# A second attention group moved back by one dense block, key scaling ahead of a weight conversion, and two steps' expert splits at fixed places

## The chip, the core and the metric

The kernel runs on one core of a Trainium2 chip. The metric is the device time of one execution in microseconds, here the median of three timed runs. A further execution was profiled; the rows below come from it.

## What is computed

A gated linear attention over 4 x 8 heads, 768 positions and 48 dimensions, then a dense layer with squared ReLU over 3072 tokens of 384 values (inner size 2048), then a routed layer in which each token goes to one of 8 experts (inner size 1024). All is in float32; the dense weights arrive as 64-bit numbers.

```
state = f[t] * state + k[t] v[t]^T;  y[t] = q[t] state      # per head
x   = relu(x @ w_in) ** 2 @ w_out                           # 3072 x 384, inner 2048
e   = argmax(x @ w_gate);  p = softmax(x @ w_gate)[e]
out = p * (relu(x @ w1[e]) @ w2[e])                         # 8 experts, inner 1024
```

## The kernel before

**Attention and dense layer.** The sequence is cut into 24 chunks of 128 tokens; three chunks make a dense group `g` of 384 tokens, 0 to 7. Each group goes through 16 blocks `i` of 128 inner columns: `moe_h` (PE, L394 in group 0 and L404 later, tile `ph`), `moe_act` (ScalarE L410 and L411 make `gg`, L415 its rounded part `gh`, VectorE L417 the rest `gl`) and, two blocks later, `moe_out` (PE, L434, three tiles `po`). The attention of group g + 1 is woven into the blocks of group g by `attention_group`, a generator that is resumed after each `moe_h` (`late` 0) and after each `moe_out` (`late` 1). For its m-th chunk it issues the scores (`pk` L256, `pa` L263) and the masked product `at` (L270) at block 5m, the decays of the next chunk (scans L215 and L224) one block later, the outputs (L299, L309, L319) two, and the scaling of the next chunk's queries and keys (`scale_qk`, VectorE L234 to L236) three blocks later. The scaled keys are the input of `pk`. At the head of the program the scaling of chunk 3 is issued by itself, behind `convert_job(2)`.

**Conversion of the weights.** In group 0 the dense weights are narrowed from 64-bit numbers by VectorE, in 16 jobs of three operations each (L166, L169, L172), two blocks' worth of `w_in` (even jobs) or `w_out` (odd jobs) at a time. Job n frees one of three staging buffers, into which SP then loads job n + 3 (L184). h(2j) and h(2j + 1) of group 0 read the tile of job 2j. When the last job is issued the staging pool is closed and a table `wgb` is loaded (L784) into its place; SP's queue has the next chunks' loads and the transposed group (`xT`, L335) behind it. From group 1 on, each weight is used as a rounded high part `w_hi` and a rest `w_lo`, and each product takes three matmuls.

**Expert steps.** The routed layer runs as 16 fixed steps on gathered tokens, of two kinds, "D" with 256 tokens and "S" with 128. A step has 8 blocks: hidden matmuls (L981, or L969 in an S step's first half), `hh` (ScalarE L985), `hl` (VectorE L986) and output matmuls two blocks later (L1001, `qo` in a D step, `qs` in an S step). The weights of a step are 8 raw tiles (`load_w`, SP, L634, `raw<-w_e`); `split_part` makes the high part on ScalarE (L612) and the rest (L613) on VectorE or, in the steps, on either VectorE or GpSimd. A split of raw tile j frees it, and `load_w` for the next step follows. Steps write their split weights alternately into two sets, `wst_[0]` (which was the dense `w_in`) and `wst_[1]` (dense `w_out`). The splits of step 0 and some of step 1 are made while the last blocks of group 7 still run. Where the splits of later steps go is planned by `split_plan`, which steps through the blocks with assumed durations; a tile is `ready` 4.0 after its release, and for step `NEARLY` (2) not before a given block of step 1, since its expert number comes from the tables that `final_tables` builds in steps 0 and 1 (`sel` L668, `pi` L672). The last group's routing (`route(7)`, L546 to L554) runs there too.

**Order.** Through the dense groups PE, ScalarE, VectorE and GpSimd run in the order of the program text (`by_hand`); SP's order, and the order of engines that are not named in a later `manual_schedule`, is the scheduler's. In steps 0 and 1 only PE was in program order.

Of the kernel before, what the change touches and what calls it, by code (L numbers as in the profile page):

```python
# [41 lines left out]
NEARLY = 2  # L42
# [14 lines left out]
def gla_moe_moe_kernel(ctx: ExitStack, tc: tile.TileContext, qk, ft, vt, w_in, w_out, w_gate, w_gateT, w_e, q, k, v, f_logit, out, dbg=None):  # L57
# [106 lines left out]
    def narrow(dst, w):  # L164
        low, high = w[..., 0], w[..., 1]
        nc.vector.tensor_scalar(  # L166
            out=dst, in0=high, scalar1=3, scalar2=0x3FFFFFFF, op0=ALU.logical_shift_left, op1=ALU.bitwise_and
        )
        nc.vector.scalar_tensor_tensor(  # L169
            out=dst, in0=high, scalar=0xC0000000, in1=dst, op0=ALU.bitwise_and, op1=ALU.bitwise_or  # L170
        )
        nc.vector.scalar_tensor_tensor(  # L172
            out=dst, in0=low, scalar=29, in1=dst, op0=ALU.logical_shift_right, op1=ALU.bitwise_or
        )
# [4 lines left out]
    def stage_job(n):  # L179
        if n < len(jobs):  # L180
            which, j = jobs[n]
            src = w_out[:, 2 * j : 2 * j + 2, :] if which else w_in[:, :, j * 256 : (j + 1) * 256]
            t = stg.tile([128, WP], I64, tag="stg", name="stg")
            nc.sync.dma_start(out=t.rearrange("p (a b) -> p a b", a=src.shape[1]), in_=src)  # L184
            staged[n] = t

    def convert_job(n):
        if n < len(jobs):
            w_raw[jobs[n]] = t = wlp.tile([128, WP], F32, tag="w", name="w_raw")
            narrow(t.bitcast(U32), staged.pop(n).bitcast(U32).rearrange("p (b two) -> p b two", two=2))  # L190
            stage_job(n + 3)
# [37 lines left out]
    def scale_qk(c):  # L229
        t, pr, _ = ld_t[c]  # L230
        tl, _ = prep_t[c]
        pairs = lambda a: a.rearrange("p (a b) -> p a b", a=4)
        qd, kd = t[:, 0], t[:, 1]
        nc.vector.tensor_tensor(out=kd, in0=kd, in1=pairs(tl[:, 1:FL])[:, :, 1:], op=ALU.mult)  # L234
        nc.vector.tensor_tensor(out=qd, in0=qd, in1=pairs(pr[:, 0 : FL - 1])[:, :, 1:], op=ALU.mult)
        nc.vector.tensor_tensor(out=pmin[0:PR], in0=pmin[0:PR], in1=tl[:, 1:FL:SEG], op=ALU.min)  # L236

    def x_tiles(g):
        xT = (
            xhp.tile([128, 3, G], F32, tag="xl", name="xT0")  # L240
            if g == 0
            else xp.tile([128, 3, G], F32, tag="xT", name="xT")
        )
        x_t[g] = xT, xp.tile([128, G], F32, tag="xT3", name="xT3")
# [93 lines left out]
    def state(c, pu):  # L338
        if pu is None:
            return  # L340
        wn = wst[(c + 1) % 2][:, :, 0:D]
        emb = prep_t[c + 1][1][:, :, None].to_broadcast([PR, 4, D])
        if c % CPB == 0:
            nc.vector.tensor_tensor(out=wn, in0=pu[0:PR], in1=emb, op=ALU.mult)
        else:
            nc.vector.tensor_tensor(out=wn, in0=pu[0:PR], in1=wst[c % 2][:, :, 0:D], op=ALU.add)
            nc.vector.tensor_tensor(out=wn, in0=wn, in1=emb, op=ALU.mult)
# [12 lines left out]
    def attention_group(g):  # L360
        for m in range(GC):
            c = g * GC + m
            b = 5 * m
            while not (yield) == (b, 1):
                pass
            if m == 0:
                x_tiles(g)
            if 4 < c + 2 < NCH:
                load_chunk(c + 2)
            scores(c)  # L370
            masked(c)
            sigmoid(c + 1)
            while not (yield) == (b + 1, 0):
                pass
            if c + 1 < NCH:
                decays(c + 1)
            while not (yield) == (b + 2, 1):
                pass
            state(c, outputs(c))
            while not (yield) == (b + 3, 0):  # L380
                pass
            if c + 1 < NCH:
                scale_qk(c + 1)
        while not (yield) == (14, 0):
            pass
        split_x(g)
        yield
# [210 lines left out]
    convert_job(1)  # L598
    decays(3)
    state(2, pu)  # L600
    convert_job(2)
    scale_qk(3)
    job = 3

    ph2 = ExitStack()
    early = {}
    rawt, xg = [], []
    wst_ = []
    ids_t, esi_t, reg_t, x_s, out_t = {}, {}, {}, {}, {}

    def split_part(hi, lo, src, eng=nc.vector):
        nc.scalar.activation(out=hi, in_=src, func=AF.Copy)  # L612
        eng.tensor_tensor(out=lo, in0=src, in1=hi.bitcast(F32), op=ALU.subtract)  # L613
# [15 lines left out]
    def load_w(s, j):  # L629
        if s >= NALWAYS:  # L630
            return
        if s not in reg_t:
            reg_t[s] = nc.sync.value_load(esi_t[s], min_val=0, max_val=NE - 1)
        nc.sync.dma_start(out=rawt[j], in_=w_e[bass.ds(reg_t[s] * 128, 128), j * WP : (j + 1) * WP])  # L634
# [66 lines left out]
    def open_right():  # L701
# [42 lines left out]
        load_x(0)  # L744
        load_x(1)

    pend = []
    rt_gen = None

# [15 lines left out]

    for g in range(NG):
        att = Piece(attention_group(g + 1)) if g + 1 < NG else None
        if g == NG - 1:
            right = open_right()
        for i in range(NF):  # L770
            ph = moe_h(g, i)
            if att:
                att.at(i, 0)
            if rt_gen and 2 <= i <= 10 and g < NG - 1:
                next(rt_gen, None)
            if g == 0 and job < len(jobs):
                convert_job(job)
                job += 1
                if job == len(jobs):
                    phs.close()  # L780
                    wgp = pha.enter_context(tc.tile_pool(name="wgp", bufs=1, side="right", reuse_waits="tile"))
                    wgb = [wgp.tile([128, NE, DM], F32, name="wgb")]
                    early["ab"] = [wgp.tile([128, NBLK + SB], F32R, name=f"ab{m}") for m in range(GC)]
                    nc.sync.dma_start(out=wgb[0], in_=w_gateT[None, :, :].to_broadcast([128, NE, DM]))  # L784
            pend.append((g, i, *moe_act(g, ph)))
            n = g * NF + i - 8
            split_job(n)
            if n == len(jobs) - 1:
                wst_.extend([[w_hi[w][:, j], w_lo[w, j]] for j in range(NP)] for w in range(2))
            if len(pend) > 2:  # L790
                done = flush_one()
                if done is not None:
                    rt_gen = route(done)
                    next(rt_gen)
            if att:
                att.at(i, 1)
            if g == NG - 1:
                if i < 2:
                    next(right, None)

                for j in {5: [0], 7: [1], 9: [2], 10: [3], 11: [4], 13: [5], 15: [6, 7]}.get(i, ()):
                    split_part(*wst_[0][j], rawt[j])
                    load_w(1, j)
                if i == 13:
                    prep_step(0, *early["x0"])
            if rt_gen and i >= 2 and (i > 10 or g == NG - 1):
                next(rt_gen, None)
        if rt_gen:
            for _ in rt_gen:
                pass  # L810
            rt_gen = None
# [130 lines left out]
        nc.vector.tensor_tensor(out=need, in0=need, in1=over[:, 1:2], op=ALU.add)  # L942
        nc.vector.scalar_tensor_tensor(out=tot, in0=need, scalar=0.0, in1=bad, op0=ALU.max, op1=ALU.add)

    early["split"], early["ready"] = [], False
    SPLITS = split_plan()


# [123 lines left out]
        if s < NEARLY:  # L1072
            next(fin, None)

    with tc.manual_schedule(engines={mybir.EngineType.PE}):
        left = run_steps(0, NEARLY, hook, flush=False)
    with tc.manual_schedule(engines={mybir.EngineType.PE, mybir.EngineType.Activation}):
        run_steps(NEARLY, NALWAYS, pend=left)
# [11 lines left out]
def split_plan():  # L1090
    slots, clock = [], 0.0
    for s, kind in enumerate(KINDS[:NALWAYS]):
        for i in range(8):
            slots.append((clock, s, i))
            clock += 2.0 if kind == "D" else 1.2
    begin = {(s, i): t for t, s, i in slots}
    ready, plan = {(1, j): 0.0 for j in range(8)}, {}

    def release(s, j, t):
        if s < NALWAYS:  # L1100
            ready[s, j] = max(t + 4.0, begin[1, 2] if s == NEARLY else 0.0)

    for t, s, i in slots:
        if KINDS[s] == "S" and i % 2:
            release(s + 1, i // 2, t)
        due = []
        for (u, j), r in ready.items():
            if (KINDS[u] == "S" and j < 4) or r > t or begin[u - 1, 2 if j == 7 else 0] > t:
                continue
            due.append((begin[u, 2 * j if j < 4 else min(2 * j - 6, 7)], u, j))  # L1110
        due.sort()
        for n, (end, u, j) in enumerate(due[:2]):
            if n and end > t + 6.0:
                break
            del ready[u, j]
            plan.setdefault((s, i), []).append((u, j))
            release(u + 1, j, t)
    return plan
# [252 lines left out]
```

## Time and profile before

| | us |
|---|---|
| median of 3 timed runs | 824.01 |
| lowest and highest | 823.91, 825.7 |
| the profiled execution | 823.52 |
| its span | 821.7 |
| PE busy | 785.1 (96% of the span) |
| VectorE, ScalarE, GpSimd busy | 548.8, 414.2, 159.9 |

Span is the time from the first to the last instruction of the profiled execution. PE is TensorE's matmul queue; a matmul counts as busy on a lower clock too, so a slow stretch doesn't show in this share.

### The profile page before, as it was taken

Reading aid. Unit: us, or ns where it says so; the run is one execution under the profiler, and the core shown is the slowest. Engines: PE = TensorE matmul, PEld = TensorE weight load, DVE = VectorE, ACT = ScalarE, POOL = GpSimd, SP = SyncE. Lnnn points to the kernel's source line nnn. Section 1 sums busy time; section 2 is a strip of 40 time slices with the busy share of each in tenths; the row PEclk is TensorE's granted clock in tenths of the full one; section 3 lists DMA queues with packets and bytes.
Section 4 is the critical chain, followed back from the end, with each engine's and each line's share of the span. In section 5 each row is a group of like instructions: output and inputs, shape, how many; then the busy total and the mean of one; then the engine's idle time right before and its main releaser. Section 6 shows DMA issues by size and latency. Waiting matters only on the chain.

```text
span 821.7 us, 15286 instructions
## 1 busy us (share of the span) xinstructions
PE 785.1 (96%) x5681; PEld 729.6 (89%) x5681; DVE 548.8 (67%) x1266; ACT 414.2 (50%) x830; POOL 159.9 (19%) x158
## 2 busy tenths in 40 slices
PE   5799999999999999999999999989999999999995
PEld 4566679999999999999999999989999899898995
DVE  7979779768768767767767654568566545656641
ACT  2233466455455454454455454753465465555651
POOL 2000000000000000000000011212656466555551
PEclk9899999999999999999999999999999999999998
DMA  9886321112131121130120015314666766758640
GB/s 266 238 266 179 126 47 52 45 53 56 43 88 38 49 63 45 46 98 25 45 69 1 2 43 205 107 59 168 238 210 223 255 218 206 268 177 277 203 143 29
DMA packets 40563, 102.09 MB, mean 124 GB/s; under 512 B 5630, under 2 KB 9442, under 8 KB 40352
## 3 DMA queue, kind: packets, MB, share of 16 engines
q1 hardware_dynamic: 36896, 91.57, 36.3%
q0 software_dynamic: 3584, 9.46, 3.1%
q8 instruction: 47, 0.77, 0.4%
q14 instruction: 36, 0.29, 0.1%
HBM read 91.31 MB, written 10.24 MB: 124 GB/s over the span
## 4 chain that ended last, share of the span: by engine, by line
PE 76%; DVE 8%; issue 6%; DMA 5%; ACT 4%; POOL 1%; SPq 0%; POOLq 0%; DVEq 0%; ACTq 0%
PE po L434 22%; PE ph L404 20%; PE qo L1001 8%; PE ph L981 8%; DVE w_lo L613 4%; PE ph L394 4%; DMA raw<-w_e 3%; PE pa L263 3%; PE py L319 3%; ACT w_hi L612 2%; PE ph L969 1%; PE py L299 1%; PE pu L309 1%; PE qs L1001 1%; DMA xT<-xT 1%
## 5 line engine op out<-in xcount | busy, mean ns | idle before, releaser
L410 ACT ACTIVATE gg<-ph 128x384 f32<-128x384 f32 x128 | 62.7, 490 | 180.8 <-PE ph L404 128.3
L417 DVE TENSOR_TENSOR gl<-gg,gh 128x384 fp32r<-128x384 f32 x112 | 63.4, 566 | 84.4 <-ACT gh L415 83.2
L404 PE MATMUL ph<-xh,w_lo 128*128 128x384 f32 x336 | 118.7, 353 | 0.9 <-ACT gg L410 0.9
L434 PE MATMUL po<-w_hi,gl 128*128 128x384 f32 x336 | 113.8, 339 | 2.2 <-DVE gl L417 2.2
L404 PE MATMUL ph<-xl,w_hi 128*128 128x384 f32 x336 | 114.4, 340 | 0.6 <-DVE xl L162 0.6
L404 PE MATMUL ph<-xh,w_hi 128*128 128x384 f32 x336 | 113.9, 339 | 0.0
L434 PE MATMUL po<-w_hi,gh 128*128 128x384 f32 x336 | 113.7, 338 | 0.0
L434 PE MATMUL po<-w_lo,gh 128*128 128x384 f32 x336 | 113.2, 337 | 0.0
L613 DVE TENSOR_TENSOR w_lo<-raw,w_hi 128x768 fp32r<-128x768 f32 x63 | 94.4, 1500 | 24.0 <-ACT w_hi L612 18.2
L613 POOL TENSOR_TENSOR w_lo<-raw,w_hi 128x768 fp32r<-128x768 f32 x49 | 91.1, 1875 | 82.8 <-ACT w_hi L612 80.4
L612 ACT ACTIVATE w_hi<-raw 128x768 fp32r<-128x768 f32 x112 | 93.8, 839 | 19.8 <-DMA raw<-w_e 19.6
L986 DVE SCALAR_TENSOR_TENSOR hl<-ph,hh 128x256 fp32r<-128x256 f32 (+1 forms) x128 | 48.8, 387 | 78.8 <-ACT hh L985 76.3
L985 ACT ACTIVATE hh<-ph 128x256 fp32r<-128x256 f32 (+1 forms) x128 | 45.2, 356 | 97.5 <-PE ph L981 72.4
L708 POOL MEMSET xg<- 128x385 f32 x4 | 1.5, 422 | 466.9 <-DVE gl L417 466.9
L981 PE MATMUL ph<-xh,w_lo 128*128 128x256 f32 x288 | 82.8, 288 | 5.9 <-DVE w_lo L613 5.9
L458 DVE SCALAR_TENSOR_TENSOR junk<-rows,wgb 128x384 f32<-128x384 f32 x144 | 80.0, 555 | 3.3
L981 PE MATMUL ph<-xl,w_hi 128*128 128x256 f32 x288 | 81.4, 283 | 0.0
L981 PE MATMUL ph<-xh,w_hi 128*128 128x256 f32 x288 | 81.1, 282 | 0.0
L411 ACT ACTIVATE gg<-gg 128x384 f32<-128x384 f32 x128 | 67.2, 525 | 4.0
L404 PEld LDWEIGHTS ph<-xh,w_lo 128*128 128x128 f32 x336 | 63.0, 187 | 6.9 <-issue 3.1
L1001 PE MATMUL qo<-w_hi,hl 128*128 128x384 f32 x192 | 66.4, 346 | 1.7 <-DVE hl L986 1.3
L434 PEld LDWEIGHTS po<-w_hi,gl 128*128 128x128 f32 x336 | 63.3, 189 | 2.8 <-DVE gl L417 2.5
(236 smaller groups left out, 1653.9 us busy)
## 6 DMA issues: line engine op xcount, KB each, us to landing
raw<-w_e SPq DMA_DIRECT2D x128, 384.0 KB
qk<-qk SPq DMA_DIRECT2D x46, 192.0 KB
v<-vt SPq DMA_DIRECT2D x24, 256.0 KB
stg<-w_in SPq DMA_DIRECT2D x8, 768.0 KB
stg<-w_out SPq DMA_DIRECT2D x8, 768.0 KB
f<-ft SPq DMA_DIRECT2D x24, 226.2 KB
xs<-rows SPq DMA_DIRECT2D x8, 577.5 KB
wgb<-w_gateT SPq DMA_DIRECT2D x1, 1536.0 KB
```

Source lines behind the costliest of these rows:

```text
L404: nc.tensor.matmul(ph, lhsT=w[:, sl], rhs=x[:, k, :], start=(n == 0), stop=(n == 8))
L410: nc.scalar.activation(out=gg, in_=ph, func=AF.Relu)
L411: nc.scalar.activation(out=gg, in_=gg, func=AF.Square)
L417: nc.vector.tensor_tensor(out=gl, in0=gg, in1=gh.bitcast(F32), op=ALU.subtract)
L434: nc.tensor.matmul(po[m], lhsT=a[:, sl], rhs=w[:, ws], start=(i == 0 and n == 0), stop=(i == NF - 1 and n == len(terms) - 1),)
L458: nc.vector.scalar_tensor_tensor(out=junk, in0=rows[:, m, 0:DM], scalar=1.0, in1=wgb[0][:, e, :], op0=ALU.mult, op1=ALU.mult, accum_out=lg ...
L612: nc.scalar.activation(out=hi, in_=src, func=AF.Copy)
L613: eng.tensor_tensor(out=lo, in0=src, in1=hi.bitcast(F32), op=ALU.subtract)
L981: nc.tensor.matmul(ph, lhsT=wslice(s, w, (i * 3 + k) * 128, 128), rhs=x[:, k, :], start=(n == 0), stop=(n == 8))
L985: nc.scalar.activation(out=hh, in_=ph, func=AF.Relu)
L986: nc.vector.scalar_tensor_tensor(out=hl, in0=ph, scalar=0.0, in1=hh.bitcast(F32), op0=ALU.max, op1=ALU.subtract)
L1001: nc.tensor.matmul(out_t[s][m], lhsT=x[:, sl], rhs=wslice(s, w, 3 * F2 + i * DM, DM), start=(i == 0 and n == 0), stop=(i == 7 and n == 2),)
```

## The change

Three edits. The attention of group 1 (in group 0's blocks) has its chunks at blocks 1, 6 and 10, not 0, 5 and 10. `scale_qk(3)` is issued ahead of `convert_job(2)`. The splits of steps 0 and 1 that fall into group 7 are listed by a table `AHEAD` (block: step and tile): all eight of step 0 and six of step 1, all on VectorE; the planner starts with what is left, step 2's tiles are ready at block 4 of step 1, and ScalarE too keeps the program order in steps 0 and 1.

```
     def attention_group(g):
         for m in range(GC):
             c = g * GC + m
-            b = 5 * m
+            b = (1, 6, 10)[m] if g == 1 else 5 * m
...
     state(2, pu)
+    scale_qk(3)
     convert_job(2)
-    scale_qk(3)
...
+    AHEAD = {4: [(0, 0)], 5: [(0, 1)], 6: [(0, 2)], 7: [(1, 0)], 8: [(0, 3), (1, 1)], 9: [(1, 2)], 10: [(0, 4)]}
+    AHEAD |= {11: [(1, 3)], 12: [(0, 5)], 13: [(1, 4)], 14: [(0, 6)], 15: [(0, 7), (1, 5)]}
...
-                for j in {5: [0], 7: [1], 9: [2], 10: [3], 11: [4], 13: [5], 15: [6, 7]}.get(i, ()):
-                    split_part(*wst_[0][j], rawt[j])
-                    load_w(1, j)
+                for t, j in AHEAD.get(i, ()):
+                    split_part(*wst_[t][j], rawt[j])
+                    if t == 0:
+                        load_w(1, j)
...
-    early["split"], early["ready"] = [], False
+    early["split"], early["ready"] = [j for js in AHEAD.values() for t, j in js if t == 1], False
...
-    with tc.manual_schedule(engines={mybir.EngineType.PE}):
+    with tc.manual_schedule(engines={mybir.EngineType.PE, mybir.EngineType.Activation}):
         left = run_steps(0, NEARLY, hook, flush=False)
...
-    ready, plan = {(1, j): 0.0 for j in range(8)}, {}
+    ready, plan = {(1, j): 0.0 for j in (6, 7)}, {}
...
-            ready[s, j] = max(t + 4.0, begin[1, 2] if s == NEARLY else 0.0)
-
+            ready[s, j] = max(t + 4.0, begin[1, 4] if s == NEARLY else 0.0)
+
+    for j in range(6):
+        release(NEARLY, j, 0.0)
```

Between chunk 2's state and chunk 3's `at`, VectorE had this order (`wst` is the attention's state, `stg` a staged weight, `qk` the chunk's queries and keys):

```order
L346 TENSOR_TENSOR wst_106<-pu,wst_105 112x4x48
L347 TENSOR_TENSOR wst_106<-wst_106,em 112x4x48
L166 TENSOR_SCALAR w_raw<-stg 128x768
L169 SCALAR_TENSOR_TENSOR w_raw<-stg,w_raw 128x768
L172 SCALAR_TENSOR_TENSOR w_raw<-stg,w_raw 128x768
L234 TENSOR_TENSOR qk_148<-qk_148,tl 112x512
L235 TENSOR_TENSOR qk_148<-qk_148,f 112x512
L236 TENSOR_TENSOR pmin<-pmin,tl 112x4
```

and now has this, with two more conversions (the same three rows) in front of `at`:

```order
L347 TENSOR_TENSOR wst_106<-wst_106,em 112x4x48
L234 TENSOR_TENSOR qk_148<-qk_148,tl 112x512
L235 TENSOR_TENSOR qk_148<-qk_148,f 112x512
L236 TENSOR_TENSOR pmin<-pmin,tl 112x4
L166 TENSOR_SCALAR w_raw<-stg 128x768
L169 SCALAR_TENSOR_TENSOR w_raw<-stg,w_raw 128x768
L172 SCALAR_TENSOR_TENSOR w_raw<-stg,w_raw 128x768
```

The three rows of the scaling went ahead of the three of conversion 2. In the same stretch PE's first dense blocks and chunk 3's scores were in this order:

```order
L394 MATMUL ph<-xT_186,w_raw 128x384 x3
L256 MATMUL pk<-ident,qk_148 128x112 x4
L263 MATMUL pa<-qk_148 128x128 x8
L394 MATMUL ph<-xT_186,w_raw 128x384 x6
L434 MATMUL po_489<-w_raw,gg 128x384
```

and are in this one now:

```order
L394 MATMUL ph<-xT_186,w_raw 128x384 x6
L256 MATMUL pk<-ident,qk_148 128x112 x4
L263 MATMUL pa<-qk_148 128x128 x8
L394 MATMUL ph<-xT_186,w_raw 128x384 x3
L434 MATMUL po_489<-w_raw,gg 128x384
```

h(0) and h(1) stand ahead of the scores, and h(2) alone behind them, where it was h(0) ahead and h(1) and h(2) behind. At the end of group 7 ScalarE had the following order. Numbered `w_hi0` tiles are of `wst_[0]` (step 0), `w_hi1` tiles of `wst_[1]` (step 1); the digit of `raw` is the tile j; `rows` is the last group's output:

```order
L415 ACTIVATE gh_5819<-gg_5816 128x384
L612 ACTIVATE w_hi1_155<-raw5_5246 128x768
L410 ACTIVATE gg_5842<-ph_5832 128x384
L411 ACTIVATE gg_5842<-gg_5842 128x384
L415 ACTIVATE gh_5845<-gg_5842 128x384
L612 ACTIVATE w_hi0_154<-raw6_5247 128x768
L612 ACTIVATE w_hi0_154<-raw7_5248 128x768
L451 ACTIVATE rows_5882<-po0_5385 128x384
```

and has this one now:

```order
L415 ACTIVATE gh_5829<-gg_5826 128x384
L612 ACTIVATE w_hi0_154<-raw6_5247 128x768
L410 ACTIVATE gg_5855<-ph_5845 128x384
L411 ACTIVATE gg_5855<-gg_5855 128x384
L415 ACTIVATE gh_5858<-gg_5855 128x384
L612 ACTIVATE w_hi0_154<-raw7_5248 128x768
L612 ACTIVATE w_hi1_155<-raw5_5246 128x768
L451 ACTIVATE rows_5894<-po0_5385 128x384
```

Step 1's split of tile 5 went from ahead of block 15's `gg` to behind its `gh`, and step 0's split of tile 6 from behind to ahead.

## Rows read from the trace of the kernel before

**Rows 1.** Page, section 1: PE's busy time, share of the span.

```profile
PE 785.1 (96%) x5681; PEld 729.6 (89%) x5681; DVE 548.8 (67%) x1266; ACT 414.2 (50%) x830; POOL 159.9 (19%) x158
```

**Rows 2.** Waits of PE: who waited for whom, total us, times, longest.

```profile
PE ph L981 <- DVE w_lo L613: 5.9, 3, 2.0
PE pk L256 <- issue: 4.8, 1, 4.8
PE po L434 <- DVE gl L417: 2.2, 1, 2.2
```

**Rows 3.** Chain that ended last, group 0: start us, us, what.

```profile
31.59 4.80 issue
37.37 2.01 PE pa L263 x16
39.38 5.45 PE ph L394 x12
44.83 1.94 PE po L434 x6
...
62.13 2.13 PE ph L394 x6
```

**Rows 4.** Half-us windows: busy by engine, PE's clock, DMA share, GB/s.

```profile
39.00:39.50 0.50, 0.50 (x5) 0.28 (x4) 0.50 (x2) 0.00 (x0) 0.00 (x0) 0.50 0.92 347
546.50:547.00 0.50, 0.50 (x4) 0.50 (x4) 0.00 (x0) 0.44 (x1) 0.00 (x0) 0.50 1.03 344
```

**Rows 5.** Timeline, group 0: start, us, instruction, idle before and releaser.

```profile
33.15 0.55 DVE L166 TENSOR_SCALAR w_raw<-stg 128x768 uint32<-128x768 uint32 x1
...
35.61 0.68 DVE L234 TENSOR_TENSOR qk<-qk,tl 112x512 f32<-112x512 f32 x1
...
36.39 0.98 PE L256 MATMUL pk<-ident,qk 112*128 112x112 f32 x4 [4.82 <-issue]
...
36.88 0.55 DVE L166 TENSOR_SCALAR w_raw<-stg 128x768 uint32<-128x768 uint32 x1
...
39.41 1.29 DVE L270 TENSOR_TENSOR at<-pa,mask 128x512 f32<-128x512 f32 x2
...
43.25 0.54 DVE L166 TENSOR_SCALAR w_raw<-stg 128x768 uint32<-128x768 uint32 x1
...
62.16 1.29 DVE L270 TENSOR_TENSOR at<-pa,mask 128x512 f32<-128x512 f32 x2 [4.62 <-PE pa L263]
```

**Rows 6.** Chain, dense layer: an undisturbed block, and the end of group 7.

```profile
496.88 1.57 PE po L434 x9
...
537.00 3.26 DMA raw<-w_e
543.49 2.92 PE po L434 x9
```

**Rows 7.** Timeline of ScalarE and VectorE, end of group 7.

```profile
540.28 0.85 ACT L612 ACTIVATE w_hi<-raw 128x768 fp32r<-128x768 f32 x1 [2.04 <-DMA raw<-w_e]
...
542.65 0.79 DVE L417 TENSOR_TENSOR gl<-gg,gh 128x384 fp32r<-128x384 f32 x1 [3.34 <-ACT gh L415]
```

**Rows 8.** Timeline, border of groups 0 and 1.

```profile
93.80 0.96 DVE L172 SCALAR_TENSOR_TENSOR w_raw<-stg,w_raw 128x768 uint32<-128x768 uint32 x1
...
94.79 0.35 SPq L784 DMA_DIRECT2D wgb<-w_gateT  x1
...
105.74 1.16 ACT L161 ACTIVATE xh<-xT 128x1152 fp32r<-128x1152 f32 x1 [7.18 <-DMA xT<-xT]
```

**Rows 9.** Timeline of PE, step 1's second half.

```profile
573.31 0.44 PE L1001 MATMUL qo<-w_hi,hl 128*128 128x384 f32 x1 [0.41 <-issue]
...
577.45 0.44 PE L1001 MATMUL qo<-w_hi,hl 128*128 128x384 f32 x1 [0.19 <-DVE hl L986]
```

**Rows 10.** Chain: output matmuls behind two of the waits for `w_lo`.

```profile
653.66 1.92 PE qs L1001 x6
...
702.67 1.05 PE qs L1001 x6
```

## The prediction

> **What bounds the kernel now.** The profile's first section is read first: PE is busy for 785.1 of 821.7 us [rows 1]. A change can therefore win only in the 37 us in which PE stands, and in the stretches in which it runs on a lower clock, where "busy" hides a loss. The list of PE's waits comes second. Its longest line is the start of the kernel, which the change doesn't touch; three of the others lie where the diff edits or close to it: 4.8 us once before `pk` (L256), 2.2 us once before `po` (L434), and 5.9 us in three waits for a `w_lo` half (L613) in the expert steps [rows 2]. Third is the chain of work that ended last, around each of these waits, and last the timeline of the engine that PE waited for.
>
> In group 0 the chain shows 4.80 us of "issue" from 31.59, then chunk 3's scores (`pa`, 2.01), the 12 matmuls of h(1) and h(2) in 5.45 us, and out(0) at 44.83 [rows 3]. Six such matmuls take 2.13 us at 62.13 [rows 3], so those 12 should take 4.26. The half-microsecond window at 39.0 tells why they don't: PE was busy and its granted clock was 0.50, 1.2 GHz instead of 2.4 [rows 4]. The wait has thus cost its length and then some more. What was late is in VectorE's timeline: `convert_job(2)` at 33.15 goes ahead of `scale_qk(3)` at 35.61, and `pk` starts at 36.39, as soon as the first of the scaling's products is there [rows 5].
>
> At the end of group 7 the same figure returns. The reload of raw tile 5 for step 1 is issued at 537.00 and takes 3.26 us [rows 6]. ScalarE has step 1's split of this tile next and sits 2.04 us until 540.28; behind it are queued block 15's `gg` and `gh`, and VectorE's `gl` comes at 542.65 [rows 7]. PE's 2.2 us before `po` is the end of this [rows 2]. The nine matmuls behind it take 2.92 us instead of the 1.57 of an undisturbed block [rows 6], and the clock still reads 0.50 at 546.5 [rows 4].
>
> **Term A, group 0.** Two edits belong together. With the scaling ahead, its first product starts at 33.15 instead of 35.61 and `convert_job(2)` starts one scaling later; from L234 at 35.61 to the next L166 at 36.88 that is 1.27 us [rows 5]. So the conversion runs from 34.42, and since it took 2.46 (33.15 to 35.61) it ends near 36.9. PE has h(0) done at 31.59 and now goes on with h(1), which uses the same converted tile: to 33.7. `pk` followed L234's start by 0.78, so it can start at 33.9, and PE waits about 0.2. `pk` and `pa` took 0.98 and 2.01 even on the low clock [rows 3, 5], so the scores end by 36.9. Then comes the one new wait: h(2) needs job 2, at about 37.0. It is as long as the scores are short of that, up to 1.2 us. h(2) takes 2.13, so out(0) starts at 39.1 instead of 44.83: 5.7 us earlier. In this sum the 4.8 of waiting is gone, 1.2 of low clock (5.45 less 4.26) and about 0.9 in the scores go, and 1.2 comes back as the new wait.
>
> Does the gain last to the end of the group? What can take it back is VectorE, which has all 16 conversions to make. It had 4.62 us idle before chunk 4's `at` at 62.16 [rows 5]. In the new order conversions 7 to 9 still stand ahead of this `at`, and the conversions that came behind two h blocks are one further on; followed through with 2.46 a conversion and 3.84 for an `at` with its scans (39.41 to 43.25, from L270 to the next conversion), chunk 4's `at` falls near 60.3, chunk 5's scores come 5.6 earlier, and conversion 15, whose last operation stands at 93.80 [rows 8], ends some 5.2 earlier. On its end hangs the border: the load of `wgb` at 94.79 and the transfers behind it on SP, among them `xT`, for which ScalarE waits 7.18 us until 105.74 [rows 8]. All these move with the conversion, so h(0) of group 1 moves by about 5.2, between 5.2 (the conversions) and 5.7 (PE). I take **5.2**.
>
> **Term B, the end of group 7.** Now each reload is given three blocks: tile 0 is split for step 0 behind block 4 and for step 1 behind block 7, and so on to tile 5 at 12 and 15. A block is about 3.2 us (two halves of nine matmuls at 1.57 [rows 6]), so 9.5 us for a subtraction and a load of 3.26. Even if the subtraction took 5 us, the tile would be there. The wait goes, 2.15 us by its row to 2.2 in the list [rows 2], with 1.35 (2.92 less 1.57) in the block behind it and another quarter of a microsecond in the first matmuls of step 0, where the clock is still at half [rows 4]: **3.8**. What it costs: the subtractions of step 1's tiles 1, 3 and 5 move from GpSimd to VectorE, three times some 1 us, in blocks in which VectorE has room; nothing on the path. At its lower end this term is 0, if the wait only moves.
>
> **Term C, steps 0 and 1.** ScalarE's program order now fixes these steps, and step 2's splits start two blocks later, behind block 4 of step 1 instead of 2. Two waits of PE of 0.41 and 0.19, behind such splits, should go [rows 9]. Against that, six small operations of `route(7)` (L548 to L554) now stand in the tables' own chain ahead of `sel` (L668), so PE's `pi` behind it may come later, by at most the six operations' own time, which I bound at 1 us. Net +0.3, from −0.4 to +0.6.
>
> The rest stays: the three waits of 1.97 for `w_lo` at the edges of the S steps [rows 2], since the plan is the same from step 5's second half on.
>
> **Sum.** 5.2 + 3.8 + 0.3 = 9.3 us off the profiled execution's 823.5: 814.2. The median of the three timed runs is 0.5 above that execution, so 814.7; I say **814.6**. What a measurement can tell from no change is about 0.2%, 1.6 us.
>
> **Rivals.**
> - *The clock falls at the new waits.* Waits of 0.2 and up to 1.2 us lie three microseconds apart at 33 to 37. The wait of 4.8 lost the clock, the one of 2.2 too, but of two alike 1.97 waits at the S steps one did (`qs` 1.92 us at 653.66) and one did not (1.05 at 702.67) [rows 10]. If it falls, 1.2 to 2.1 of term A comes back: about 816.4.
> - *The remaining waits are drawn anew.* Of those two alike waits PE's clock fell at one, and everything ahead of both now moves by 9 us. A fall costs at least 0.9 us by the two `qs` rows [rows 10] and at most the 1.6 of the block in group 7 (1.35 and 0.25, above). One fall fewer gives 813, one more 816. The Trainium skill, "TensorE: Matmul & The Clock Gate", section "Part 1: The HAM clock gate", says that the chip's watch on activity runs freely, not tied to the kernel's start, and that its outcome varies from run to run; the two `qs` rows agree.
> - *The wait at the end of group 7 only moves.* If DMA queues hold a reload longer than 9.5 us, or ScalarE is late elsewhere, term B falls away: 818.4. For it speaks that the chain runs through a reload there; against it that this one landed 3.26 us after its issue, and only the place of its use was too early [rows 6, 7].
> - *The border takes some of A.* The transfers behind conversion 15 may share queues with the next chunk's: 1 to 3 us back, about 816.5.
> - *Slower.* ScalarE's order is now fixed in steps 0 and 1, so that a `hh` can stand behind a split that waits for its load, as `gg` did in group 7. There one such wait cost 3.75. Step 2's eight loads are issued only when the tables are known. Three such waits would cost 11.3, more than the 9.3 gained: 825.9; from three on this decides. Against it, the same splits wait already and cost PE only 0.41 and 0.19 [rows 9], and they come later now.
>
> **How the numbers follow.** My forecast (A and B nearly whole) 0.46; the remaining waits drawn otherwise, to one side or the other, 0.12; clock at the new waits 0.15; B lost 0.10; border 0.08; slower 0.04; 0.05 for mixtures, some of which end near no change. The range goes from 812.4 (A at 5.7, one fall of the clock fewer) to 818.4 (B lost), which leaves out some 2 in 10. Faster 0.93, same 0.03, slower 0.04.
>
> **What would show it.** Term A: PE's 4.8 before `pk` gone from the list of waits, a new one of some 1.2 before L394 for `convert_job(2)`, the clock at 1.00 at 39, out(0) near 39.1, the load of `wgb` near 89.5. Term B: no wait for block 15's `gl`, no ScalarE wait for a raw tile of over half a microsecond in group 7, nine `po` matmuls in 1.57 everywhere. Term C: no `qo` waits in step 1's second half. I am wrong if a new line in PE's waits is longer than 2 us, if the half-speed clock shows between 33 and 42, or if the first `px` of step 2 comes less than 8 us earlier than now.

## The result

The changed kernel's median is 818.13 us (seven runs, 815.55 to 821.14) against 825.20 for the kernel before (seven runs, 823.91 to 828.35): a ratio of 0.9911, 95% interval 0.9885 to 0.9936, or 7.1 us between the medians. The forecast was 814.6 in a range of 812.4 to 818.4; so the time lies near the range's upper edge, and the forecast gain of 9.4 (from 824.01, the median known then) was 2.3 too large. The profiled execution took 818.23 with a span of 816.3, so 5.4 less in span than the one before. Line numbers of the changed kernel are up to 4 higher in the expert steps (L985 for the hidden matmuls, L1005 for the output matmuls).

The list of PE's waits of the changed kernel answers to [rows 2]:

```profile
PE ph L985 <- DVE w_lo L613: 5.9, 3, 2.0
PE qo L1005 <- DVE hl L990: 2.4, 7, 1.3
PE pi L672 <- DVE sel L668: 1.4, 2, 1.0
PE ph L394 <- DVE w_raw L172: 1.4, 1, 1.4
PE ph L404 <- ACT gg L410: 1.2, 1, 1.2
```

The 4.8 in front of `pk` and the 2.2 in front of `po` are gone. New are 1.4 for the conversion, which was forecast at up to 1.2, and three lines got longer: `qo`, `pi`, and the border of groups 0 and 1. Before the change these three were:

```profile
PE qo L1001 <- DVE hl L986: 1.3, 7, 0.2
PE ph L404 <- ACT gg L410: 0.9, 1, 0.9
PE pi L672 <- DVE sel L668: 0.8, 2, 0.4
```

The timeline of group 0 answers to [rows 5]:

```profile
33.12 0.68 DVE L234 TENSOR_TENSOR qk<-qk,tl 112x512 f32<-112x512 f32 x1
...
33.91 0.57 PE L256 MATMUL pk<-ident,qk 112*128 112x112 f32 x4 [0.43 <-PE ph L394]
...
34.40 0.55 DVE L166 TENSOR_SCALAR w_raw<-stg 128x768 uint32<-128x768 uint32 x1
...
37.08 2.17 PE L394 MATMUL ph<-xT,w_raw 128*128 128x384 f32 x6 [1.37 <-DVE w_raw L172]
...
39.09 2.10 PE L434 MATMUL po<-w_raw,gg 128*128 128x384 f32 x6
```

The scaling runs first, `pk` follows its first product by 0.79, conversion 2 starts 1.28 later, and out(0) stands at 39.09: the forecast said 39.1. At the border, the timeline answers to [rows 8]:

```profile
89.21 0.35 SPq L786 DMA_DIRECT2D wgb<-w_gateT  x1
...
100.49 1.16 ACT L161 ACTIVATE xh<-xT 128x1152 fp32r<-128x1152 f32 x1 [7.51 <-DMA xT<-xT]
...
102.09 0.45 PE L404 MATMUL ph<-xh,w_lo 128*128 128x384 f32 x1 [1.24 <-ACT gg L410]
```

`xh` moved by 5.25 (105.74 to 100.49): term A arrived at the size it was given, 5.2. But two half-microsecond windows, which answer to [rows 4], show what came behind it:

```profile
39.00:39.50 0.50, 0.50 (x3) 0.27 (x2) 0.50 (x2) 0.21 (x1) 0.00 (x0) 1.00 0.98 406
104.00:104.50 0.50, 0.50 (x3) 0.50 (x2) 0.31 (x1) 0.50 (x2) 0.00 (x0) 0.50 0.13 33
```

The clock is 1.00 at 39, as forecast, and 0.50 at 104, behind the border's wait. There the kernel before, whose first matmul of group 1 stands at 107.33, had kept it:

```profile
109.00:109.50 0.50, 0.50 (x4) 0.50 (x3) 0.50 (x1) 0.50 (x2) 0.00 (x0) 1.00 0.00 0
```

The chain at the end of group 7 answers to [rows 6]:

```profile
531.36 1.57 PE po L434 x9
532.93 1.60 PE ph L404 x9
534.52 4.72 PE po L434 x27
```

The last 27 output matmuls run at 1.57 for nine, without a gap. Term B is there.

A table of intervals between six places makes the profiles comparable; each number is the difference of two starts in a timeline, in us. "pt" is the first transpose of the last group's routing, "pi" the first matmul behind the tables' `sel`, "px" the first transpose of step 2.

| kernel profiled | h(0) to out(0) | to h(0) of group 1 | to pt | to pi | to px | to the end |
|---|---|---|---|---|---|---|
| before | 15.30 | 62.66 | 440.44 | 18.64 | 14.32 | 240.97 |
| after | 9.75 | 63.00 | 438.04 | 20.18 | 14.74 | 241.25 |

So 5.6 is won in group 0 and 2.4 between the border and pt, and 2.0 is lost in steps 0 and 1. The experiments ask which edit does which, and why it wasn't 3.8 at the second place and a gain at the third.

### The profile page after: what moved, and what is told of

Read it like the earlier page. It is cut to its first block, busy times and chain, and to the rows that moved or that the text cites. A ratio compares the mean times of both kernels' runs of the same rounds, so it can differ in the third digit from the quotient of the medians.

```text
span 816.3 us, 15279 instructions
## 1 busy us (share of the span) xinstructions
PE 782.6 (96%) x5681; PEld 727.6 (89%) x5681; DVE 548.8 (67%) x1269; ACT 414.5 (51%) x830; POOL 154.4 (19%) x155
## 4 chain that ended last, share of the span: by engine, by line
PE 81%; DVE 7%; issue 5%; DMA 3%; ACT 2%; POOL 1%; POOLq 0%; SPq 0%; DVEq 0%; ACTq 0%
PE po L434 24%; PE ph L404 23%; PE ph L985 8%; PE qo L1005 8%; DVE w_lo L613 4%; PE ph L394 3%; PE pa L263 3%; PE py L319 3%; PE ph L973 1%; PE py L299 1%; DMA raw<-w_e 1%; PE pu L309 1%; ACT w_hi L612 1%; DMA xT<-xT 1%; PE qs L1005 1%
## 5 line engine op out<-in xcount | busy, mean ns | idle before, releaser
L613 POOL TENSOR_TENSOR w_lo<-raw,w_hi 128x768 fp32r<-128x768 f32 x46 | 85.3, 1869 | 104.1 <-PE pc L501 51.3
L985 PE MATMUL ph<-xh,w_lo 128*128 128x256 f32 x288 | 82.8, 287 | 5.9 <-DVE w_lo L613 5.9
L458 DVE SCALAR_TENSOR_TENSOR junk<-rows,wgb 128x384 f32<-128x384 f32 x144 | 79.9, 555 | 3.3
L985 PE MATMUL ph<-xl,w_hi 128*128 128x256 f32 x288 | 81.2, 282 | 0.0
L985 PE MATMUL ph<-xh,w_hi 128*128 128x256 f32 x288 | 81.0, 281 | 0.0
L1005 PE MATMUL qo<-w_hi,hl 128*128 128x384 f32 x192 | 66.2, 345 | 2.4 <-DVE hl L990 2.4
L1005 PE MATMUL qo<-w_hi,hh 128*128 128x384 f32 x192 | 64.9, 338 | 0.0
```

The costliest lines, as they stand in the source:

```text
L458: nc.vector.scalar_tensor_tensor(out=junk, in0=rows[:, m, 0:DM], scalar=1.0, in1=wgb[0][:, e, :], op0=ALU.mult, op1=ALU.mult, accum_out=lg ...
L985: nc.tensor.matmul(ph, lhsT=wslice(s, w, (i * 3 + k) * 128, 128), rhs=x[:, k, :], start=(n == 0), stop=(n == 8))
L1005: nc.tensor.matmul(out_t[s][m], lhsT=x[:, sl], rhs=wslice(s, w, 3 * F2 + i * DM, DM), start=(i == 0 and n == 0), stop=(i == 7 and n == 2),)
```

## The experiments

Each group of four ran on one chip, with the kernel before timed beside it; its median was 819.77, 825.25 and 820.11 in the three groups, so only ratios to it, and intervals within a profile, are compared across groups. The last interval, from px to the end, can't be compared across groups either, as the last experiment shows.

**Group 0 alone.** The first two edits of the change, on the kernel before:

```
+            b = (1, 6, 10)[m] if g == 1 else 5 * m
...
+    scale_qk(3)
     convert_job(2)
-    scale_qk(3)
```

> Group 0's two edits alone (chunks of group 1 one block later, scaling ahead of conversion 2), all else as before. My theory: out(0) at 39.1 instead of 44.8, wgb's load near 89.2, so 5.6 us less at the group border, and 5.6 less at the end unless the clock falls at one more or one fewer of the remaining waits (1.7 us each): 5.6 below the kernel before, 3.9 to 7.3 with one fall. Rival (the clock at the border always falls once the border comes earlier): 3.9 below before in every run, the border's first matmuls at half clock in the trace.

Measured: 815.52 against 819.77, ratio 0.9941 (0.9920 to 0.9962), 4.3 less. Intervals: 9.75, 62.72, 440.53, 18.65, 15.92. Group 0 gives 5.6 in the profile, which the interval of the times (3.1 to 6.6) includes, the border's clock held, and the rest to pt is unchanged. So the rival that it must fall there is out. From pi to px this execution is 1.6 longer than before: PE waited 2.5 there for ScalarE's `o`.

**The scaling alone,** and **the scores alone:** one of the two edits each.

> The kernel before with the scaling ahead of conversion 2 and nothing else. h(1) then covers conversion 2, and PE waits only in front of pk, some 2.3 us instead of 4.8. My theory: out(0) about 39.9 if the clock holds, 41.6 if it falls: 3 to 4.8 below before. Rival (the place of the scores is what counts, the scaling alone does nothing): out(0) stays near 44.7.

> The kernel before with the attention of group 1 at blocks 1, 6 and 10 and nothing else. pk still waits for the scaling behind conversion 2 until 36.4, 2.7 us after h(1); h(2) then has its tile. My theory: out(0) about 40.3 if the clock holds, 42 if it falls: 2.7 to 4.5 below before, so either edit alone brings most of term A and both together 1 to 3 us more. Rival (the scaling's place is what counts): out(0) stays near 44.7.

Measured: the scaling alone 821.38 against 825.25, 0.9964 (0.9942 to 0.9987); the scores alone 824.83, 0.9984 (0.9965 to 1.0002), not clear of no change. From h(0) to out(0) they took 10.28 and 13.73 where both together take 9.75. The row on `pk` in the list of PE's waits with the scaling alone:

```profile
PE pk L256 <- issue: 2.4, 1, 2.4
```

and with the scores alone:

```profile
PE pk L256 <- issue: 2.9, 1, 2.9
```

Almost alike, but behind the 2.9 the clock fell for 6.8 us from 36.7, and behind the 2.4 it held. With the scores alone the expected "42 if it falls" was 43.80, of which 0.7 is a later start of h(0); with the scaling alone "39.9 if the clock holds", 10.5 behind h(0), was 10.28 behind it. The scaling's place is worth 5.0 of the 5.6, the scores' 0.5 once the scaling is right.

**The splits alone, ScalarE's order fixed, and with it free.** Everything but group 0's edits; in the second kernel this line stays as it was before:

```
-    with tc.manual_schedule(engines={mybir.EngineType.PE, mybir.EngineType.Activation}):
+    with tc.manual_schedule(engines={mybir.EngineType.PE}):
         left = run_steps(0, NEARLY, hook, flush=False)
```

> The fixed places, the plan and ScalarE's program order in steps 0 and 1, with group 0 as before. My theory: the wait for gl at the end of group 7 and the low clock behind it go (3.8), and steps 0 and 1 give back 1.9: 1.9 below before. Rival (the steps' loss was chance in the one profiled execution): 3.8 to 4.1 below before, no wait of over 0.5 in front of pi and none of 1.3 in front of qo.

> The fixed places and the plan with group 0 as before and ScalarE's order in steps 0 and 1 left to the scheduler: term B by itself. My theory: 3.8 below before at the end of group 7 and nothing given back in the steps, pi 18.6 after pt: 3.8 below before, 0.9954. Rival (the gain of the fixed places is given back in the steps whoever orders ScalarE): 2 below or less, as with the fixed order.

Measured: fixed 818.38 against 819.77, 0.9984 (0.9967 to 1.0001); free 818.44 against 820.11, 0.9974 (0.9957 to 0.9990). From h(0) of group 1 to pt both took 436.4 instead of 440.5: term B is 4.1 us, whoever orders ScalarE. The times show only 1.4 and 1.7 of it, so most is given back behind pt, in each of these two executions at another place. With the order fixed, pt to pi takes 20.19 instead of 18.64, but pi to px 13.17; the sum, 33.36, is hardly more than the 32.96 and 33.41 of the kernel before. What is missing lies behind px: 239.13, where the other three profiles of this group have 235.8 to 236.6, with a wait of 1.97 for `w_lo` at 647.87 and the half clock from 648.5. That the splits cause this is not shown. With the order free, 18.69 and 16.86: ScalarE meets step 2's splits ahead of `o` while their loads are still on the way, as its timeline shows, and PE waits 1.79 for it:

```profile
569.04 0.84 ACT L612 ACTIVATE w_hi<-raw 128x768 fp32r<-128x768 f32 x1 [1.28 <-DMA raw<-w_e]
569.79 0.56 ACT L1017 ACTIVATE o<-qo,gate 128x384 f32<-128x384 f32 x1
...
570.40 0.47 PE L1005 MATMUL qo<-w_hi,hl 128*128 128x384 f32 x1 [1.79 <-ACT o L1017]
```

The clock then falls at 570.8. My expectation of 3.8 for the free order was wrong: nothing is lost in front of pi, but 2 us or more go between pi and px in this execution. The new places of the splits are not shown to be the reason: PE's wait for `o` is 2.5 with group 0 alone and 2.0 with the scores alone, where the splits are as before, and 0.8 and 0.4 in the two changed kernels below whose ScalarE is free.

**The changed kernel with ScalarE free,** and **with the plan's block 2** (`begin[1, 2]` again), ScalarE fixed.

> The changed kernel with ScalarE's order in steps 0 and 1 left to the scheduler, as before the change. My theory (the fixed order is what loses in the steps: ex stands three blocks later, and three hh in a row start only at 570.9): ex is back ahead of block 2's hh, the wait in front of pi is 0.4 again, the 1.3 in front of qo is gone, first px of step 2 some 1.9 earlier than in the changed kernel: about 1.9 below it. Rival (the later place of step 2's splits is what loses): the same time as the changed kernel.

> The changed kernel with step 2's tiles ready from block 2 of step 1 in the plan, as before the change, ScalarE's order still fixed. My theory: the splits now stand ahead of hh that PE needs and wait for their loads: no gain, up to 1 us above the changed kernel, and the wait in front of pi stays near 1.0. Rival (the later place is what loses): 1 to 2 us below the changed kernel.

Measured: 811.97 and 811.47 against 819.77, ratios 0.9903 (0.9879 to 0.9927) and 0.9890 (0.9863 to 0.9917). Neither is clear of the changed kernel's 0.9911 or of the other. Pt to pi: 18.63 with ScalarE free, 20.18 with block 2. So the 1.54 in front of pi belongs to the fixed order and not to the plan's later block. That half of my theory stood; the forecast difference in the time of about 1.9 did not show.

**The changed kernel again.**

> The changed kernel once more, beside the others of this group on one chip. My theory: the place at 571 where three hh start late (1.3 us of PE) was chance in the first profile, while the 1.55 us by which pi comes later after group 7 than before are in the order and return; pi stands 20.2 after the last group's first pt. About 0.991 of the kernel before. Rival (both are in ScalarE's fixed order): both return.

Measured: 816.45 against 825.25, 0.9905 (0.9872 to 0.9937). Intervals 9.76, 63.17, 438.10, 20.19, 13.28. What is the order's (pi at 20.19, and the border's half clock, at 105.3) came back; the 1.3 in front of `qo` did not. In the first profile ScalarE started three `hh` late there:

```profile
560.31 0.39 PE L672 MATMUL pi<-sel,slot 96*128 96x18 f32 x2 [0.96 <-DVE sel L668]
...
570.88 0.94 ACT L989 ACTIVATE hh<-ph 128x256 fp32r<-128x256 f32 x3 [4.44 <-PE ph L985]
...
571.77 0.44 PE L1005 MATMUL qo<-w_hi,hl 128*128 128x384 f32 x1 [1.32 <-DVE hl L990]
```

The first of them had its input from PE more than 4 us earlier. The second profile shows a like pause of 3.0 that costs PE next to nothing; the other profiles with the order fixed show none. What ScalarE waited for stays open.

**`ex` early.** ScalarE's order fixed as in the change, but the last group's `ex`, ScalarE's operation (L546) ahead of that routing's last six on VectorE, is issued right behind `d`:

```
         nc.vector.tensor_tensor(out=oh, in0=rev, in1=bc(rm), op=ALU.is_equal)
+        if g == NG - 1:
+            ex = sm.tile(GN, F32, tag="ex", name="ex")
+            nc.scalar.activation(out=ex, in_=d, func=AF.Sigmoid)
         yield
...
-        ex = sm.tile(GN, F32, tag="ex", name="ex")
-        nc.scalar.activation(out=ex, in_=d, func=AF.Sigmoid)
+        if g < NG - 1:
+            ex = sm.tile(GN, F32, tag="ex", name="ex")
+            nc.scalar.activation(out=ex, in_=d, func=AF.Sigmoid)
```

> The changed kernel with its fixed order of ScalarE, but ex of the last group's routing issued right behind d, so that it stands behind block 1's hh as before. My theory (ex alone is what makes pslot and pi late, since VectorE's six operations behind it fall among the tables' operations): pi 18.6 after pt instead of 20.2, 1.5 below the changed kernel, about 0.989 of before. Rival (the hh's own fixed places are what loses): pi stays at 20.2.

Measured: 813.36 against 820.11, 0.9912 (0.9889 to 0.9936). Pt to pi took 19.83: `ex` is 0.35 of the 1.54, and my theory that it is all of it falls. What may be the rest is seen in the timeline of GpSimd and VectorE of this kernel:

```profile
547.32 1.85 POOL L617 TENSOR_TENSOR w_lo<-raw,w_hi 128x768 fp32r<-128x768 f32 x1 [51.27 <-PE pc L504]
...
547.49 1.71 DVE L557 TENSOR_SCALAR ss<-ss 128x3 f32<-128x3 f32 x1
```

The same timeline of the changed kernel has the same pair:

```profile
546.66 1.85 POOL L613 TENSOR_TENSOR w_lo<-raw,w_hi 128x768 fp32r<-128x768 f32 x1 [51.27 <-PE pc L501]
...
547.03 1.52 DVE L511 TENSOR_TENSOR sl<-sl,oh 128x24 f32<-128x24 f32 x1
```

An operation on 128x3 or 128x24 elements, 0.17 us elsewhere, takes 1.5 to 1.7 and ends as GpSimd's subtraction for step 1's tile 7 ends. The fixed order put this split behind block 2 of step 0, where VectorE is in the middle of the routing. Before, GpSimd had it until 551.75, and VectorE's first operation on the routing's logits came behind it:

```profile
549.94 1.81 POOL L613 TENSOR_TENSOR w_lo<-raw,w_hi 128x768 fp32r<-128x768 f32 x1 [6.64 <-ACT w_hi L612]
...
551.93 0.18 DVE L485 COPY lg<-pl 128x24 f32<-128x24 f32 x1 [1.07 <-PE pl L484]
```

All six profiles with the order fixed show such a pair; none of the eight with it free does. The Trainium skill, "SBUF — State Buffer", section "SBUF: two separate sides", states that the two engines share a pair of ports which one holds for the whole instruction; for `sl`, with two inputs in SBUF, the trace agrees, and of `ss`, with one, the page speaks only if it runs in a two-port mode, which no row here shows. That this one subtraction is the remaining 1.2, and that moving it would bring them back, was read from these rows and not tried.

**The table later, ScalarE free,** and **the table later, `ex` early.** On the changed kernel, `wgb` is not loaded by SP ahead of `xT` but by ScalarE behind the split of group 1's `xT`:

```
                 att.at(i, 0)
+            if g == 0 and i == 14:
+                nc.scalar.dma_start(out=wgb[0], in_=w_gateT[None, :, :].to_broadcast([128, NE, DM]))
...
-                    nc.sync.dma_start(out=wgb[0], in_=w_gateT[None, :, :].to_broadcast([128, NE, DM]))
```

> The changed kernel with two edits: ScalarE's order in steps 0 and 1 left to the scheduler, and wgb's load issued by ScalarE behind the split of group 1's xT, so that xT is not queued behind 1.5 MB. My theory (the border waits for xT only because wgb goes first, and the longer wait there lets the clock fall): PE's waits of 1.2 and 0.6 at the border and the half clock behind them go, first matmul of group 1 at about 100.3, 3.5 less by group 1's blocks, and pi 18.6 after pt: about 5 below the changed kernel, 0.985 of before. Rival (the border waits for something else, or the table then comes late for the routing): the first matmul of group 1 stays at 102, or VectorE's L458 waits and the gain is gone.

> The same with wgb's load issued by ScalarE behind the split of xT. My theory: first matmul of group 1 at 100.3 after the start of this kernel's h(0) at 29.3, no half clock there, pi 18.6 after pt: as the kernel with the table later and ScalarE free, 0.984 of before. Rival: one of the two gives back, 0.986 to 0.99.

Measured: 810.75 against 825.25, 0.9840 (0.9814 to 0.9866), where the changed kernel on the same chip took 816.45; and 809.11 against 820.11, 0.9857 (0.9834 to 0.9881). Both are faster than either kernel. The second differs from `ex` early by the table alone, and on the same chip takes 4.2 less (809.11 against 813.36): this is the table's own worth. The border in the timeline of the first:

```profile
89.45 1.33 SPq L335 DMA_DIRECT2D xT<-xT  x2
...
93.57 1.16 ACT L161 ACTIVATE xh<-xT 128x1152 fp32r<-128x1152 f32 x1 [0.66 <-DMA xT<-xT]
93.81 0.38 ACTq L777 DMA_DIRECT2D wgb<-w_gateT  x1
...
100.32 0.64 PE L404 MATMUL ph<-xh,w_lo 128*128 128x384 f32 x1
```

`xT` is there seven microseconds earlier, PE goes into group 1 without waiting, at 100.32 as expected, and the clock falls nowhere before 803. From out(0) to pt it takes 497.1 where the changed kernel takes 501.0. VectorE's first use of the table (L458) stands at 111.42, in the changed kernel at 115.44, so the table is not late.

**The kernel before again,** profiled once.

> The kernel before, profiled once more beside the others of this group. My theory (the clock falls or holds anew at each wait in each execution): the waits of 4.8 and 2.2 are there again and the clock falls behind both, but at the three waits for w_lo not necessarily at the same one as in the first profile. Rival (it is fixed by the program): low at 35, 544 and 653 again and nowhere else.

Measured: 818.81, the clock low at 34.9 and 543.5 only. The last interval, from px to the end, is 235.86 instead of the 240.97 of the first profile, with the same instructions. At the first edge of an S step, the timeline of GpSimd and VectorE in the first profile reads:

```profile
649.46 1.82 POOL L613 TENSOR_TENSOR w_lo<-raw,w_hi 128x768 fp32r<-128x768 f32 x1
649.48 2.62 DVE L613 TENSOR_TENSOR w_lo<-raw,w_hi 128x768 fp32r<-128x768 f32 x1 [0.45 <-issue]
```

and in this one:

```profile
648.75 0.96 DVE L613 TENSOR_TENSOR w_lo<-raw,w_hi 128x768 fp32r<-128x768 f32 x1 [0.44 <-ACT w_hi L612]
...
650.62 1.85 POOL L613 TENSOR_TENSOR w_lo<-raw,w_hi 128x768 fp32r<-128x768 f32 x1
```

Within 0.02 us of each other, VectorE's subtraction takes 2.62; 0.7 us earlier and well ahead of GpSimd's, 0.96. PE's waits for `w_lo` are 5.9 in the one and 1.0 in the other. So part of what I took for a fixed cost of three edges is a matter of timing. It goes with the group of runs and not with the kernel. The first two profiles and the four of the group whose kernel before took 825.25 have all three waits at 1.97 or 1.98, and 239.5 to 241.3 from px to the end; the eight of the other two groups, 819.77 and 820.11, have 0.7 to 3.9 of such waits in sum, and 235.8 to 239.1. The 5 us between these medians are of the size of this difference. What makes VectorE's and GpSimd's subtractions meet in some groups and not in others stays open.

## Why the prediction held, and where it was off

The median lies in the stated range, and the interval of the ratio, 5.3 to 9.5 us off 825.20, includes the 9.4 that was forecast. That is in part luck. The range ended at 818.4 for the case that term B is lost; B was not lost, and what brought the time near that edge was a fall of the clock at the border and a loss in the steps. One of my own signs of being wrong was met: the first `px` of step 2 came 5.7 earlier (580.73 to 575.05), and not 8.

- **Term A** was right in mechanism and size: out(0) at 39.09 for 39.1, the border 5.25 earlier for 5.2, and the rival that the clock falls at the new waits did not come: in all eight profiles with both edits it is up at out(0).
- **The border** was mis-sized. I carried 5.2 across it and counted nothing for a fall of the clock at the wait that remains there; of my two rivals that bear on it, "drawn anew" named the S edges alone, and "the border takes some of A" gave 1 to 3 back, but by shared queues. PE's wait for `gg` there is 0.9 to 1.1 in the profiles without a fall of the clock (before twice, group 0 alone, the scaling alone, the splits alone twice) and 1.2 to 1.6 in those with one (the changed kernel twice, and with ScalarE free, with block 2, with `ex` early, and the scores alone). Up to pt the splits alone save 4.1 and the changed kernel 2.4: the fall costs 1.6 to 1.7. Taking the wait away brings it back: with the table later it is 435.8 from h(0) of group 1 to pt, twice. Why the wait is longer in the changed kernel than with group 0's edits alone, which give the same program up to there, stays open: from the issue of the table to `xh` it took 11.00 with those alone and 11.22 to 11.66 in the five profiles of changed kernels that load the table first, and each is one execution.
- **Term B** was right, 4.1 for 3.8: the reload no longer holds ScalarE, whose splits in group 7 have no wait for a raw tile in the changed kernel's profile.
- **Term C** had a cost wrong: +0.3 was forecast, and by pi it is −1.54 in the four profiles with the fixed order and `ex` in its place, −1.2 in the two with `ex` early. I had seen `ex` and its operations (0.35) and missed, as I read the rows above, the split of step 1's tile 7, which GpSimd now does while VectorE is on the routing. From pi to px the fixed order, with later splits or with block 2, takes 13.1 to 13.3 in five of six profiles, the free order 14.1 to 17.2, so it gives back 1 or more. From pt to px those five take 33.0 to 33.5, the kernel before 32.96 and 33.41: in sum about nothing, where +0.3 was forecast. In the first profile of the changed kernel the open pause came on top: 34.92, and Term C's own sign, no wait for `qo` in step 1's second half, failed there with 1.32.
- **The sum:** 9.3 by the terms; less 1.6 at the border, and less 2.3 (first profile, 34.92 against 32.96 with +0.3 forecast) or 0.8 (second) in the steps, with 0.3 more in B, gives 5.7 or some 7 up to px, and 7.1 was timed. The slower rival, three ScalarE waits for loads, did not come in the fixed order.

## What to carry to other kernels

A stretch in which the bottleneck engine stands is worth its length plus the half clock that may follow it, as the 4.8 in front of `pk` was. So look at each remaining wait on that engine, not only at those that the edit names. A large load that nobody needs yet should not stand in the queue ahead of a small one for which the bottleneck waits; moving it here was worth 4.2 us by itself. Where an order is fixed by hand, check what each helper engine does beside the chain that is critical there: beside one subtraction on GpSimd a 0.17 us operation took 1.5.

## What the runs showed of the hardware

The clock is not a function of the program and its waits alone. The changed kernel's two profiles both have three waits of 1.97 or 1.98 at the S edges; behind the third the clock fell in the first profile:

```profile
741.79 0.58 PE L985 MATMUL ph<-xh,w_lo 128*128 128x256 f32 x1 [1.97 <-DVE w_lo L613]
743.00:743.50 0.50, 0.50 (x5) 0.50 (x4) 0.00 (x0) 0.50 (x1) 0.00 (x0) 0.50 1.02 403
```

and held in the second:

```profile
741.42 0.39 PE L985 MATMUL ph<-xh,w_lo 128*128 128x256 f32 x1 [1.97 <-DVE w_lo L613]
743.00:743.50 0.50, 0.50 (x5) 0.50 (x4) 0.50 (x2) 0.50 (x2) 0.00 (x0) 1.00 1.15 369
```

Of the 18 such waits in the six profiles that have them at all three edges it fell behind three. The prediction's two `qs` rows are of one execution and could not show this. A wait of 2.4 in front of `pk` kept it and one of 2.9 lost it for 6.8 us. And two engines' subtractions on 128x768 elements that start within 0.02 us of each other take 1.82 and 2.62, where VectorE's takes 0.96 alone.
